# Five wq chunks kept between uses, and the place of w1 used for K, for wo and as three lent ring slots

## The chip, the cores and the metric

The kernel runs on one core of one Trainium2 chip. The metric is the device time of one execution in microseconds (us), as the median over runs. A profile of one execution stands beside it; its span runs from the first to the last instruction.

## What is computed

Two kinds of layer alternate, attention A and MLP B, twice each with the same weights, for one token of 1024 features, forward and backward:

```
x = A_x
x = x + A(layernorm(x));  x = x + B(layernorm(x))
x = x + A(layernorm(x));  x = x + B(layernorm(x))
A: q = x @ wq (32 heads of 128); scores against the last 4096 rows of k_cache (4 kv heads);
   softmax; sum over v_cache; @ wo
B: h = x @ w1 + b1;  act = h * tanh(softplus(h));  act @ w2
outputs: x, and the gradients of A_x, k_cache, v_cache, wq, wo, w1, b1, w2 for a given grad_out
```

wq is 1024 x 4096, wo 4096 x 1024, w1 1024 x 3584, w2 3584 x 1024, all bf16. The gradients of the two caches are full size (4 x 32768 x 128 each); all but the last 4096 rows of each are zeros.

## The kernel before

Weights pass through SBUF in chunks of 128 partitions x 4096 bf16, 1.05 MB each: wq and wo are eight chunks each, w2 seven. `ring_t` has eight such slots. K and V live whole in `KT` and `VS`, w1 whole in `W1` (128 x 8 x 3584, loaded as eight pieces of 0.92 MB). In the list below the number is the use: 0 first forward, 1 second forward (and wo's and w2's second use serve forward and backward both), 2 and 3 backward.

The class `Ring` (L40 to L80) sets the order of all loads. `want` appends a load to a list; `pump` walks the list in order and issues each load on SyncE's queue. A load with a place of its own (`own`: V, w1) is issued without a slot, any other takes the first free slot, and the walk stops when none is free. `release` gives a slot back and pumps, `keep` renames a chunk so that it stays for a later use. `release` is called while the program is being built, behind the instructions that use the chunk, and the loads that it lets go are put into the program at that point. The schedule is written out by hand: every engine runs its instructions in the order in which they were put, and waits between engines follow from who last wrote or read a place before that point.

The list (L254 to L270): K, q0, V, the first two w2 chunks (`EARLY_2`), o0, w1, the rest of w2, q1, o1, q2, w2 again, o3, q3. `KEEP_Q` (L251) names the wq chunks that stay from use 0 to use 1, `KEEP_Q2` (L252) those that stay from use 2 to use 3; q1 and q3 load only the others.

The stages, in order: K is transposed into `KT` (`kt_transposes`, L561, frees K's slots). `attn_fwd` (L462) multiplies wq chunk by chunk (L473), scores and softmax, then wo (L553); in the first attention each wo chunk is released after its products, in the second wo stays for the backward. `mlp_fwd` (L595) multiplies w1 (L601) and makes the activation `AC` (L628). Then w2 (L697 to L706): for each chunk the products forward (`mlp_out`, L653) and, in `rows_chunk` (L447), two blocks per chunk turned on TensorE (L431), evicted (L287 on ScalarE) and multiplied (L443) for the gradient; the other two blocks are row products on VectorE (L408). Products run two behind their transposes (`later`, L415), and a chunk's release is put behind its products, so a slot comes back at the end of the next chunk. The last w2 chunk is finished in `last_da` (L710), inside the second attention.

The backward runs `attn_bwd(1)` (wo, V, K, then wq in its `dn` part, L877 to L903), the second w2 stage (L1077 to L1082), `dn_b0` (L804, w1), and `attn_bwd(0)`. A wq chunk that was turned in use 2 and kept needs no turning in use 3 (`turned_q`, L893). From then on `W1` is used for rows and as staging: `stage_free` (L946) starts with three staging places in it, and VS, KT and the ring slots are added as they come free. Last, all weight gradients are made from rows (`work`), evicted into staging places and stored.

Zeros for the cache gradients, 56 stores of 1.05 MB, are issued on POOL's queue at fixed points (`zeros`, L240); with a second argument POOL first copies one word of that tile, so that it waits for it. `dn1` (L1123) has the last of them.

Of the kernel before, what the change touches and what calls it, by code (L numbers as in the profile page):

```python
# [15 lines left out]
P = 128  # L16
HQ = 32
DH = 128
D = 1024
# [6 lines left out]
TS = W // P  # L26
SLOT = 4096
# [10 lines left out]
class Ring:  # L38
# [12 lines left out]
    def pump(self):  # L51
        while self.pending:
            key, src, shape, own = self.pending[0]
            if own is None:
                if not self.free:
                    return
                s = self.free.popleft()
                n = 1
                for k in shape[1:]:
                    n *= k  # L60
                dst = self.slots[s][:, 0:n]
                if len(shape) == 3:
                    dst = dst.rearrange("p (a b) -> p a b", a=shape[1])
                self.where[key] = (s, dst)
            else:
                dst = own
            self.pending.popleft()
            self.nc.sync.dma_start(dst, src)

# [6 lines left out]

    def release(self, key):
        s, _ = self.where.pop(key)
        self.free.append(s)
        self.pump()  # L80


# [1 line left out]
def kernel(  # L84
# [50 lines left out]
    W1 = sb([P, TD, F], BF16, "W1")  # L135
# [56 lines left out]
    AC = sb([P, TF, 2], BF16, "AC")  # L192
# [13 lines left out]
    ring = Ring(nc, [ring_t[:, i, :] for i in range(8)])  # L206
    wq_v = A_wq.rearrange("(t p) j -> p t j", p=P)

    wo_v = A_wo.rearrange("(c p k) d -> p c k d", p=P, k=4)
# [3 lines left out]
    def kv_src(cache, g):  # L213
        return cache[0, g, ZR:, :].rearrange("(p t) d -> p t d", p=P)
# [2 lines left out]
        for t in ts:  # L217
            ring.want(("q", k, t), wq_v[:, t, :], [P, J])

    def want_o(k, cs=range(8)):  # L220
        for c in cs:
            ring.want(("o", k, c), wo_v[:, c], [P, 4, D])

    def want_2(k, cs=range(7)):
        for c in cs:
# [4 lines left out]
    for out_t in (out_2, out_3):  # L230
        for g in range(G):
            dst = out_t[0, g, 0:ZR, :].rearrange("(p r) d -> p (r d)", p=P).rearrange("p (r c) -> p r c", c=ZC)
# [7 lines left out]
    def zeros(n, after=None):  # L240

        if after is not None and zjobs:
            nc.gpsimd.tensor_copy(pz[0:1, pz_n[0] % 16:pz_n[0] % 16 + 1], after[0:1, 0:1])
            pz_n[0] += 1
        for _ in range(n):
            if zjobs:
                dst = zjobs.pop()
                nc.gpsimd.dma_start(dst, zt[:])  # L248


    KEEP_Q = (6, 7)  # L251
    KEEP_Q2 = (5, 6, 7)  # L252
    EARLY_2 = (0, 1)
    for g in range(G):  # L254
        ring.want(("K", g), kv_src(A_k_cache, g), [P, TS, P])
    want_q(0)
    for g in range(G):
        ring.want(("V", g), kv_src(A_v_cache, g), None, own=VS[:, g])
    want_2(0, EARLY_2)
    want_o(0)  # L260
    for t in range(TD):
        ring.want(("1", t), w1_v[:, t, :], None, own=W1[:, t, :])
    want_2(0, [c for c in range(7) if c not in EARLY_2])
    want_q(1, [t for t in range(8) if t not in KEEP_Q])
    want_o(1)
    want_q(2)
    want_2(1)
    want_o(3)
    want_q(3, [t for t in range(8) if t not in KEEP_Q2])
    ring.pump()  # L270
# [166 lines left out]
    def mv_open():  # L437

        fresh[0] = True
# [22 lines left out]
    def attn_fwd(l, x, st, first, wo_hook, q_hook=None):  # L462
# [7 lines left out]
        for t in range(TD):  # L470
            ch = ring.get(("q", l, t))
            for h in range(HQ):
                nc.tensor.matmul(q_ps[:, h:h + 1], lhsT=ch[:, h * P:(h + 1) * P], rhs=NA[:, t, l:l + 1],  # L473
                                 start=(t == 0 and h == 0), stop=(t == TD - 1), skip_group_check=True)
            if l == 0 and t in KEEP_Q:
                ring.keep(("q", 0, t), ("q", 1, t))
# [118 lines left out]
    def mlp_fwd(l, x, st):  # L595
        name = f"B{l}"
        n32, rstd = ln_fwd(x, st, NB[:, :, l], name)
        h_ps = MV[:, 192:192 + TF]
        for t in range(TD):
            for fb in range(TF):  # L600
                nc.tensor.matmul(h_ps[:, fb:fb + 1], lhsT=f_block(W1[:, t], fb), rhs=NB[:, t, l:l + 1],  # L601
                                 start=(t == 0 and fb == 0), stop=(t == TD - 1), skip_group_check=True)

        taken = []

        def col(n):
            if n == "mp":
                return sb([P, TF], FP32, f"{n}_{name}")
            taken.append(n)
            return mlp_t[:, (len(taken) - 1) * TF:len(taken) * TF]  # L610

        h, nh, z, w, m, om, A, B, num, den, t_, = (col(n) for n in "h nh z w m om A B num den t".split())
        V = nc.vector
        V.tensor_tensor(out=h[:], in0=h_ps, in1=b1c[:], op=ALU.add)

        V.scalar_tensor_tensor(out=nh[:], in0=h[:], scalar=-1.0, in1=h[:], op0=ALU.mult, op1=ALU.min)
        nc.scalar.activation(z[:], nh[:], ACT.Exp)
        nc.scalar.activation(w[:], nh[:], ACT.Exp, scale=2.0)
        V.tensor_scalar(out=m[:], in0=h[:], scalar1=0.0, scalar2=None, op0=ALU.is_ge)
        V.tensor_scalar(out=om[:], in0=h[:], scalar1=0.0, scalar2=None, op0=ALU.is_lt)  # L620
        V.tensor_tensor(out=A[:], in0=m[:], in1=w[:], op=ALU.max)
        V.tensor_tensor(out=B[:], in0=om[:], in1=w[:], op=ALU.max)
        V.scalar_tensor_tensor(out=num[:], in0=z[:], scalar=2.0, in1=A[:], op0=ALU.mult, op1=ALU.add)
        V.scalar_tensor_tensor(out=den[:], in0=B[:], scalar=2.0, in1=num[:], op0=ALU.mult, op1=ALU.add)
        V.reciprocal(den[:], den[:])
        V.tensor_tensor(out=t_[:], in0=num[:], in1=den[:], op=ALU.mult)
        if l == 0:
            V.tensor_tensor(out=AC[:, :, l], in0=h[:], in1=t_[:], op=ALU.mult)  # L628

        def deriv():  # L630

            mp, sg, s2 = col("mp"), col("sg"), col("s2")
            V.tensor_scalar(out=s2[:], in0=z[:], scalar1=1.0, scalar2=None, op0=ALU.add)
            V.reciprocal(s2[:], s2[:])
            V.tensor_tensor(out=sg[:], in0=m[:], in1=z[:], op=ALU.max)
            V.tensor_tensor(out=sg[:], in0=sg[:], in1=s2[:], op=ALU.mult)
            V.tensor_tensor(out=mp[:], in0=t_[:], in1=t_[:], op=ALU.mult)
            V.tensor_scalar(out=mp[:], in0=mp[:], scalar1=-1.0, scalar2=1.0, op0=ALU.mult, op1=ALU.add)
            V.tensor_tensor(out=mp[:], in0=mp[:], in1=h[:], op=ALU.mult)
            V.tensor_tensor(out=mp[:], in0=mp[:], in1=sg[:], op=ALU.mult)  # L640
            V.tensor_tensor(out=mp[:], in0=mp[:], in1=t_[:], op=ALU.add)
            return mp

        def act_late():
            V.tensor_tensor(out=AC[:, :, l], in0=h[:], in1=t_[:], op=ALU.mult)

        return dict(n32=n32, rstd=rstd, deriv=deriv, act_late=act_late)
# [36 lines left out]
    def early_da(k):  # L684
        c, tt = EARLY_2[k // 4], k % 4
        r = 4 * c + tt
# [6 lines left out]

    x1, st1, sA0 = attn_fwd(0, x0, st0, True, wo_hook0)
    sB0 = mlp_fwd(0, x1, st1)
    mp0 = sB0["deriv"]()
    y_ps = MV[:, 256:256 + TD]  # L697
    mv_open()
    for c in range(7):
        ch = ring.get(("2", 0, c))  # L700
        mlp_out(0, ch, c, y_ps)
        if c in EARLY_2:
            ring.release(("2", 0, c))
# [47 lines left out]
    dnp = sb([P, TD], FP32, "dnp")  # L751
# [52 lines left out]
    def dn_b0(g):  # L804
        bcast(lambda c: DHC[:, c, 0:1], STAY)
        mv_open()
        for t in range(TD):
            rowdot(W1[:, t, 0:STAY * P], [LB[0][:, 0:512]], 512, dnp[:, t:t + 1], True)
            mv(W1[:, t, STAY * P:], TF - STAY, TP[:, t:t + 1], lambda i: DHC[:, STAY + i, 0:1], True)
            if t == 2:  # L810
                rowize(GB, TD, 96, 0)
                take_back("AC", 96, NOFF)
                take_back("NB", 64, 0)
                take_back("OC", 32, NOFF)
                take_back("NA", 0, 0)
            if t == 4:
                rowize_f()
        return ln_bwd(dnp, sB0["n32"], sB0["rstd"], g, "B0")
# [107 lines left out]
    def dn3(t):  # L926
        if t % 2:
            w1_rest(1)
        if t == 5:
            zeros(1, dnp[:, t:t + 1])  # L930

    g2 = attn_bwd(1, sA1, g3, ("o", 1), ("q", 2), KEEP_Q2,
                  dict(do=lambda c: conv(2), dp=dp3, dq=dq3, dn=dn3))


    W1S = W1[:].rearrange("p t f -> p (t f)")
    ROWS = W1S[:, 0:5120]
    NOFF = 1024
    rf = W1S[0:7, 5120:6144]
    rt = W1S[0:64, 6144:6656].rearrange("p (k i) -> p k i", k=4)  # L940
# [2 lines left out]
    DOST = W1S[:, 11008:11264]  # L943

    TWIN = W1S[:, 11264:16384]
    stage_free = deque(W1S[:, 16384 + i * SLOT:16384 + (i + 1) * SLOT] for i in range(3))  # L946
    rt_n = [0]

    def rowize(cols, n, base, off):
# [136 lines left out]
    w1_rest(len(w1_units))  # L1086
    zeros(2, dh0)
    g1 = dn_b0(g2)
    nc.vector.tensor_copy(GA[:, :, 0], g1[:])
    zeros(2, g1)  # L1090

# [30 lines left out]

    def dn1(t):  # L1123
        if t in (3, 6, 7):
            zeros(2 if t < 7 else 1, dnp[:, t:t + 1])
        if t == 4:
            twins()
        if t == 5:
            todo[0].append(units_cols(0, 8, out_4))
# [9 lines left out]
    nc.vector.tensor_copy(g0b[:], g0[:])  # L1139
    store_rows(g0b[:], TD, out_1[0, 0, :])  # L1140
    stage_free.extendleft(ring_t[:, i, :] for i in range(8))

    way.close()
    late = ctx.enter_context(tc.tile_pool(name="late", bufs=1, space=bass.MemoryType.PSUM))
# [42 lines left out]
```

## Time and profile before

| | us |
|---|---|
| median of 3 runs | 462.74 (462.68 to 465.34) |
| span of the profiled execution | 460.6 |
| busy: TensorE / VectorE / ScalarE / GpSimd | 337.2 / 261.3 / 228.2 / 38.6 |

The core moved 183.59 MB (83.94 MB read from HBM, 98.62 MB written), 399 GB/s over the span; SyncE's queue carried 123.94 MB and POOL's queue, the zeros, 58.72 MB. The time around the profiled span is not listed; the median of the runs is 2.1 us above that span. In the profile, PE is TensorE, PEld its weight load, DVE VectorE, ACT ScalarE, SPq the instructions of SyncE's queue. The rows of a time line have the start, the duration, the engine, the line, what is written and read, a count, and in brackets the idle time before and what ended it. The granted clock is TensorE's, as a share of full speed. Many matmuls of a row are pipelined, and some records can be missing.

### The profile page before, as it was taken

Reading aid. Unit: us, or ns where it says so; the run is one execution under the profiler, and the core shown is the slowest. Engines: PE = TensorE matmul, PEld = TensorE weight load, DVE = VectorE, ACT = ScalarE, POOL = GpSimd, SP = SyncE. Lnnn points to the kernel's source line nnn. Section 1 sums busy time; section 2 is a strip of 40 time slices with the busy share of each in tenths; the row PEclk is TensorE's granted clock in tenths of the full one; section 3 lists DMA queues with packets and bytes.
Section 4 is the critical chain, followed back from the end, with each engine's and each line's share of the span. In section 5 each row is a group of like instructions: output and inputs, shape, how many; then the busy total and the mean of one; then the engine's idle time right before and its main releaser. Section 6 shows DMA issues by size and latency. Waiting matters only on the chain. (4 is left out here: it accounts for less than half of the span.)

```text
span 460.6 us, 14273 instructions
## 1 busy us (share of the span) xinstructions
PE 337.2 (73%) x6385; PEld 275.3 (60%) x6385; DVE 261.3 (57%) x517; ACT 228.2 (50%) x263; POOL 38.6 (8%) x85
## 2 busy tenths in 40 slices
PE   4836435597678788599879898897896876677950
PEld 3736435497668787599779898787791121112530
DVE  6505731383150149678428786475485987878860
ACT  2502001064035369378128573283267988778850
POOL 4000000000111320100210101102111000000000
PEclk9955555555555569799559855597595555555555
DMA  8999999999999999999999999979999999999995
GB/s 340 420 419 419 419 420 416 422 388 392 393 422 424 418 414 414 406 384 386 376 424 334 407 387 371 414 264 408 424 420 421 419 425 421 427 424 419 408 407 227
DMA packets 28379, 183.59 MB, mean 399 GB/s; under 512 B 3706, under 2 KB 3734, under 8 KB 9494
## 3 DMA queue, kind: packets, MB, share of 16 engines
q1 hardware_dynamic: 20162, 123.94, 67.0%
q0 software_dynamic: 8064, 58.72, 30.7%
q8 instruction: 50, 0.82, 0.7%
q14 instruction: 11, 0.09, 0.0%
q10 hardware_dynamic: 92, 0.02, 0.0%
HBM read 83.94 MB, written 98.62 MB: 396 GB/s over the span
## 5 line engine op out<-in xcount | busy, mean ns | idle before, releaser
L287 ACT COPY ring<-BIG 128x1024 bf16<-128x1024 bf16 x73 | 72.2, 1013 | 40.4 <-PE BIG L431 37.7
L431 PE MATMUL BIG<-ident_bf,ring 128*128 128x128 bf16 x872 | 80.0, 252 | 3.8 <-DMA ring<-in_A_wo_dram 2.0
L431 PEld LDWEIGHTS <-ring 128*128 128x128 bf16 x952 | 69.8, 114 | 5.2 <-DMA ring<-in_A_wo_dram 2.3
L995 PE MATMUL wide<-W 2*128 2x512 bf16 x228 | 48.5, 601 | 19.0 <-DVE ring L284 3.6
L408 DVE CUSTOM_DVE_ANT_0 junk<-ring,SC 128x1024 bf16<-128x1024 bf16 x38 | 46.2, 1216 | 4.5 <-DMA ring<-in_A_wo_dram 1.7
L995 PEld LDWEIGHTS <-W 2*128 2x128 bf16 x240 | 10.9, 103 | 54.5 <-issue 53.8
L443 PEld LDWEIGHTS <-ring 128*128 128x128 bf16 x1024 | 38.2, 100 | 4.6 <-ACT ring L287 4.4
L287 ACT COPY KT<-BIG 128x1024 bf16<-128x1024 bf16 x22 | 21.8, 1015 | 32.3 <-PE BIG L582 30.9
L287 ACT CAST ring<-wide 128x1024 bf16<-128x1024 f32 (+1 forms) x38 | 35.2, 998 | 4.9 <-PE wide L995 4.0
L284 DVE COPY ring<-BIG 128x1024 bf16<-128x1024 bf16 x36 | 24.8, 691 | 20.3 <-PE BIG L431 13.1
L284 DVE CAST ring<-wide 128x1024 bf16<-128x1024 f32 (+1 forms) x26 | 30.2, 1200 | 5.7 <-PE wide L995 5.2
L248 POOL DMA_DIRECT2D out_dram<-zt x56 | 29.6, 534 | 6.3 <-DMA out_dram<-zt 5.6
L553 PE MATMUL MV<-OC,ring 128*128 128x1 bf16 x512 | 16.6, 166 | 15.2 <-DMA ring<-in_A_wo_dram 12.6
L287 ACT COPY W<-BIG 128x1024 bf16<-128x1024 bf16 x20 | 18.9, 1151 | 15.7 <-PE BIG L766 15.7
L553 PEld LDWEIGHTS <-ring 128*128 128x128 bf16 x512 | 16.0, 106 | 16.0 <-DMA ring<-in_A_wo_dram 13.2
L284 DVE CAST VS<-wide 128x1024 bf16<-128x1024 f32 (+1 forms) x18 | 21.0, 1190 | 4.1 <-PE wide L995 3.1
L473 PE MATMUL MV<-NA,ring 128*128 128x1 bf16 x512 | 15.0, 165 | 10.9 <-DMA ring<-in_A_wq_dram 10.0
L601 PE MATMUL MV<-NB,W 128*128 128x1 bf16 x448 | 16.2, 172 | 9.2 <-DMA W<-in_B_w_dram 6.5
L408 DVE CUSTOM_DVE_ANT_0 junk<-ring,DSX 128x1024 bf16<-128x1024 bf16 x18 | 22.0, 1224 | 0.6
L601 PEld LDWEIGHTS <-W 128*128 128x128 bf16 x448 | 15.9, 118 | 9.8 <-DMA W<-in_B_w_dram 7.2
L1046 PE MATMUL wide<-W 32*128 32x256 bf16 x128 | 20.4, 403 | 1.4 <-ACT W L287 0.8
L473 PEld LDWEIGHTS <-ring 128*128 128x128 bf16 x512 | 14.3, 103 | 11.6 <-DMA ring<-in_A_wq_dram 10.6
(256 smaller groups left out, 539.1 us busy)
## 6 DMA issues: line engine op xcount, KB each, us to landing
out_dram<-zt POOLq DMA_DIRECT2D x56, 1024.0 KB, 12.7
ring<-in_A_wq_dram SPq DMA_DIRECT2D x27, 1024.0 KB
ring<-in_A_wo_dram SPq DMA_DIRECT2D x24, 1024.0 KB
ring<-in_B_w_dram SPq DMA_DIRECT2D x14, 1024.0 KB
out_dram<-ring SPq DMA_DIRECT2D x9, 1024.0 KB
W<-in_B_w_dram SPq DMA_DIRECT2D x8, 896.0 KB
ring<-in_A_k_cache_dram SPq DMA_DIRECT2D x4, 1024.0 KB
VS<-in_A_v_cache_dram SPq DMA_DIRECT2D x4, 1024.0 KB
```

Source lines behind the costliest of these rows:

```text
L248: nc.gpsimd.dma_start(dst, zt[:])
L284: nc.vector.tensor_copy(dst, src)
L287: nc.scalar.copy(dst, src)
L408: nc.vector.tensor_tensor_reduce(out=out, in0=a, in1=vec, scale=1.0, scalar=acc if i else 0.0, op0=ALU.mult, op1=ALU.add, accum_out=acc)
L431: nc.tensor.transpose(b[:, i * P:(i + 1) * P], block(w, i) if block else w[:, i * P:(i + 1) * P], ident_bf[:])
L443: nc.tensor.matmul(out, lhsT=w[:, i * P:(i + 1) * P], rhs=rhs_of(i), start=fresh[0], stop=last and i == n - 1, skip_group_check=True)
L473: nc.tensor.matmul(q_ps[:, h:h + 1], lhsT=ch[:, h * P:(h + 1) * P], rhs=NA[:, t, l:l + 1], start=(t == 0 and h == 0), stop=(t == TD - 1), ...
L553: nc.tensor.matmul(y_ps[:, dd:dd + 1], lhsT=ch[:, tt, dd * P:(dd + 1) * P], rhs=OC[:, h, l:l + 1], start=(h == 0 and dd == 0), stop=(h == ...
L601: nc.tensor.matmul(h_ps[:, fb:fb + 1], lhsT=f_block(W1[:, t], fb), rhs=NB[:, t, l:l + 1], start=(t == 0 and fb == 0), stop=(t == TD - 1), ...
L995: nc.tensor.matmul(b[:, 512 * i:512 * i + 512], lhsT=R[at:at + 2, lo:lo + P], rhs=R[at:at + 2, ro + 512 * i:ro + 512 * i + 512], start=Tru ...
L1046: nc.tensor.matmul(b[:, k * 256:(k + 1) * 256], lhsT=RT[32 * g:32 * g + 32, a, tp, :], rhs=YS[32 * g:32 * g + 32, :], start=True, stop=Tru ...
```

## The change

K is loaded into four of seven homes, 4096 columns each, that lie in `W1`, instead of into ring slots. The first seven chunks of o0 go into the same seven homes, the eighth into a ring slot. Both `KEEP_Q` and `KEEP_Q2` name five chunks. A load with its own place is now entered in `where`, and its release gives no slot back. After `dn_b0`, `ring.lend` adds three slots in `W1` (columns 16384 to 28671) to the ring; the staging list starts empty, and gets these three places at the end. Two zero stores are put after the first MLP's activation, and two fewer stand in `dn1`.

```diff
     def pump(self):
         while self.pending:
             key, src, shape, own = self.pending[0]
-            if own is None:
+            if own is not None:
+                self.where[key] = (None, own)
+                dst = own
+            else:
                 if not self.free:
                     return
                 s = self.free.popleft()
...
                 self.where[key] = (s, dst)
-            else:
-                dst = own
             self.pending.popleft()
             self.nc.sync.dma_start(dst, src)
...
     def release(self, key):
         s, _ = self.where.pop(key)
-        self.free.append(s)
+        if s is not None:
+            self.free.append(s)
+        self.pump()
+
+    def lend(self, slots):
+
+        self.free.extend(range(len(self.slots), len(self.slots) + len(slots)))
+        self.slots.extend(slots)
         self.pump()
...
-    def want_o(k, cs=range(8)):
+    def want_o(k, cs=range(8), homes=()):
         for c in cs:
-            ring.want(("o", k, c), wo_v[:, c], [P, 4, D])
+            own = homes[c].rearrange("p (k d) -> p k d", k=4) if c < len(homes) else None
+            ring.want(("o", k, c), wo_v[:, c], [P, 4, D], own)
...
-    KEEP_Q = (6, 7)
-    KEEP_Q2 = (5, 6, 7)
+    KEEP_Q = (3, 4, 5, 6, 7)
+    KEEP_Q2 = (3, 4, 5, 6, 7)
     EARLY_2 = (0, 1)
+    W1S = W1[:].rearrange("p t f -> p (t f)")
+    homes = [W1S[:, i * SLOT:(i + 1) * SLOT] for i in range(7)]
     for g in range(G):
-        ring.want(("K", g), kv_src(A_k_cache, g), [P, TS, P])
+        ring.want(("K", g), kv_src(A_k_cache, g), None, own=homes[g].rearrange("p (t d) -> p t d", t=TS))
     want_q(0)
     for g in range(G):
         ring.want(("V", g), kv_src(A_v_cache, g), None, own=VS[:, g])
     want_2(0, EARLY_2)
-    want_o(0)
+    want_o(0, homes=homes)
...
     sB0 = mlp_fwd(0, x1, st1)
+    zeros(2, AC[:, 0, 0:1])
...
-    stage_free = deque(W1S[:, 16384 + i * SLOT:16384 + (i + 1) * SLOT] for i in range(3))
+    lent = [W1S[:, 16384 + i * SLOT:16384 + (i + 1) * SLOT] for i in range(3)]
+    stage_free = deque()
...
     g1 = dn_b0(g2)
+    ring.lend(lent)
...
         if t in (3, 6, 7):
-            zeros(2 if t < 7 else 1, dnp[:, t:t + 1])
+            zeros(1, dnp[:, t:t + 1])
...
     stage_free.extendleft(ring_t[:, i, :] for i in range(8))
+    stage_free.extendleft(lent)
```

More of the change, by code (lines that the diff above doesn't have):

```diff
@@ L933 @@
                   dict(do=lambda c: conv(2), dp=dp3, dq=dq3, dn=dn3))
-    W1S = W1[:].rearrange("p t f -> p (t f)")
     ROWS = W1S[:, 0:5120]
```

## The prediction

> **What bounds the kernel now.** I read the page's first two parts, then a table by stretches, then the time lines of TensorE and of SyncE's queue between 60 and 120 us and around 260 to 310 us, where the ring of eight slots is used.
>
> ```profile
> PE 337.2 (73%) x6385; PEld 275.3 (60%) x6385; DVE 261.3 (57%) x517; ACT 228.2 (50%) x263; POOL 38.6 (8%) x85
> DMA  8999999999999999999999999979999999999995
> ```
>
> No engine is busy three quarters of the span, and the DMA engines are busy in every slice but the first and last and the one near 300 us. By stretches (columns: stretch, its length, busy us of PE, PEld, DVE, ACT, POOL, granted clock, DMA share, GB/s):
>
> ```profile
> 2.00:87.00 85.00, 45.29 (x1142) 42.03 (x1143) 32.53 (x75) 13.64 (x18) 4.15 (x4) 0.62 1.01 417
> 87.00:111.00 24.00, 19.47 (x454) 19.17 (x452) 17.04 (x50) 13.20 (x16) 0.00 (x0) 0.50 0.99 392
> 111.00:202.00 91.00, 71.25 (x1545) 66.03 (x1543) 37.60 (x116) 42.41 (x52) 15.63 (x32) 0.64 1.01 413
> 262.00:300.00 38.00, 34.61 (x699) 33.52 (x698) 26.53 (x63) 17.74 (x20) 2.47 (x6) 0.51 0.99 392
> 350.00:450.00 100.00, 70.57 (x394) 24.81 (x393) 77.67 (x69) 80.77 (x91) 0.00 (x0) 0.50 1.02 419
> ```
>
> Up to 87 us TensorE only follows the loads. From 87 to 350 us the order of the compute sets the pace, and DMA is full there because zero stores are handed out to fill it. From 350 us stores of 39.9 MB (98.62 MB written less 58.72 MB of zeros) set it. The time line of TensorE shows the place the change touches first:
>
> ```profile
> 69.29 1.01 PE L553 MATMUL MV<-OC,ring 128*128 128x1 bf16 x32 [1.47 <-DMA ring<-in_A_wo_dram]
> 72.73 2.01 PE L601 MATMUL MV<-NB,W 128*128 128x1 bf16 x56 [1.36 <-DVE NB L353]
> 75.83 1.09 PE L601 MATMUL MV<-NB,W 128*128 128x1 bf16 x28 [1.09 <-DMA W<-in_B_w_dram]
> 86.71 1.10 PE L601 MATMUL MV<-NB,W 128*128 128x1 bf16 x28 [1.08 <-DMA W<-in_B_w_dram]
> 90.21 2.70 PE L653 MATMUL MV<-AC,ring 128*128 128x1 bf16 x96 [2.41 <-DVE AC L628]
> 115.62 1.55 PE L473 MATMUL MV<-NA,ring 128*128 128x1 bf16 x52 [1.34 <-DMA ring<-in_A_wq_dram]
> ```
>
> wo's products (L553) end at 70.3, before w1's loads land, one each 2.18 us, the last at 86.7. The w2 stage starts at 90.2 with its chunks there. SyncE's issues:
>
> ```profile
> 60.76 8.83 SPq L68 DMA_DIRECT2D W<-in_B_w_dram  x8
> 71.48 20.08 SPq L68 DMA_DIRECT2D ring<-in_B_w_dram  x5
> 92.08 18.34 SPq L68 DMA_DIRECT2D ring<-in_A_wq_dram  x6
> ```
>
> **What goes.** Three loads of wq for the second forward use and two for the last: 5 x 1.05 MB, at the 420 GB/s of a loading stretch 12.5 us of DMA. That counts only if DMA is not left idle as long. Two zero stores move from L1125 to the first MLP; their bytes stay.
>
> **Step 1: what w1's place does to wo.** Loads are put into the program when `pump` runs. The first use of wq frees three slots. Two go to the early w2 chunks, the third to wo's eighth chunk; wo's first seven have homes in W1 and need no slot. So behind the third release nothing stops `pump`: w1's eight loads follow at once, before the products of wo stand in the program. In the kernel before, wo's last four loads needed slots that wo's own products freed, which put w1 behind them. Now those products (L553) read places that w1's loads wrote last by the program's order, so they must wait for these loads (and multiply w1's words). Home c holds parts of w1's chunks c and c+1. w1's loads themselves still wait only for wo's to land, which the stream orders anyway, so they land as before, the last at 86.7. wo's seventh chunk runs at 86.7, its eighth ends at 88.7 instead of 70.3. Behind it on TensorE are the norm and all of L601: norm 2.4 us (70.3 to 72.7), eight w1 chunks without waits 8.0 us (2.01 for two), activation 2.4 us (87.8 to 90.2). AC is ready at 101.5 instead of 90.15: **+11.4 us**. DMA idles meanwhile: w2's third chunk takes the eighth wo chunk's slot at 88.7, and nothing more is free. Cost bounds: 0 (if w1's loads waited for the products) and 11.4. I take 11.4, because L601's rows show that a reader of W1 waits for each load of what it reads.
>
> **Step 2: three slots in the first w2 stage.** Before, six circulated. A chunk's TensorE work is 3.0 us (rows at clock 0.5: 94.43, 97.46, 100.45), and its slot is given back at the end of the next chunk's. What a load takes from issue to use: the queue's row for the last wq load and the L473 row above give 110.09 to 115.62, 5.5 us; zero stores into a quiet queue land after 6.2 us.
>
> ```profile
> 110.09 0.33 SPq L68 DMA_DIRECT2D ring<-in_A_wq_dram  x1
> DMA to landing us min/median/max: 6.2/8.9/11.8
> ```
>
> I take 5.7 us for one alone. From AC at 101.5: the early chunks free slots at 102.6 and 103.5; the fourth and fifth chunk are loaded beside the two new zero stores (POOL's copy 0.67 us and 0.53 us each to issue; nothing waits on POOL until the second attention, L482). Each queue gets about half, as the four transfers are 10 us of data from 104: they land at 110.7 and 116. Then chunk by chunk: fourth 110.7 to 113.7 (frees the third's slot: sixth chunk at 119.5), fifth 116 to 119 (seventh chunk at 124.6), sixth 119.5 to 122.5 (wq's first), seventh from 124.6, norm and `last_da` to 131.3 as before (103.43 to 110.0). wq's second load is issued at 129, its third at 131.4 when `last_da` gives the last slot back: usable at 134.7 and 137. Five kept chunks follow at 0.9 us: q is done at 142.6 where it was 119.4. So +23.2 with step 1, **11.8 of it from the ring**. Bounds: without the zeros beside the loads the same walk ends at 138.2 (7.4); with every load 1 us longer at 146. Wo's loads for the second attention then start late too, but so does their use, by the same time.
>
> The Trainium skill, DMA: Bandwidth & Descriptors (Anatomy of one DMA), gives 2.0 us plus bytes over 436 GB/s, an estimate of 4.4 us for one chunk. By that, the two walks of this and the next step would shorten by about 6 us, and the sum below be 478; the row above has 5.5, and I stay with it.
>
> **111 to 262 us:** same instructions, same zeros, eight slots free for wo: only moved.
>
> **Step 3: three slots in the second w2 stage.** There wq's third use gives back three slots, not five:
>
> ```profile
> 260.67 0.95 PE L653 MATMUL MV<-AC,ring 128*128 128x1 bf16 x32
> 266.39 0.33 SPq L68 DMA_DIRECT2D ring<-in_B_w_dram  x1
> 275.06 1.22 DVE L408 CUSTOM_DVE_ANT_0 junk<-ring,SC 128x1024 bf16<-128x1024 bf16 x1 [1.58 <-DMA ring<-in_B_w_dram]
> ```
>
> The first release comes at 266.39, and that load, beside three zero stores, was usable 8.7 us later. Before, it was the sixth chunk; now it is the fourth, wanted at 269.2 and there at 274.5. The fifth (issued 269.4) follows at 277.5. The sixth is issued at 277.5 and there at 283.2, the seventh at 286.2, which started at 278.1 before: **+8.2 us** (6 if the zeros have drained first, 10 if all loads take 8.7).
>
> **Step 4: lent slots.** `lend` stands after the MLP's gradient; the loads are behind the row copies (L792 up to 294) on SyncE. wo's fourth to sixth chunk come about when wanted, the last two earlier than now: the waits of 0.62 and 1.40 us at 310.9 and 314.4 shrink. **-1** (0 to -2).
>
> **Step 5: two more wq chunks already turned.** Six transposes of 0.65 us with their evictions and three of DVE's 0.69 us copies go from 331 to 346; DVE's row products (1.27 us each) end the stage near 343.4: **-3** (-2 to -4).
>
> **Step 6: the tail.** Before, some 4.3 zero stores (10.5 us) were left at 350.2. Now two are gone and two wq loads fewer stand ahead, so they are through about when the first store can begin, 4.3 us after the norm. 39.9 MB at 420 GB/s are 95 us, then 5 us as before (455.5 to 460.6): 104.3 instead of 110.4, **-6.1**. ACT and DVE need about 80 us there and stay covered.
>
> **Sum:** 460.6 + 23.2 + 8.2 - 1 - 3 - 6.1 = 481.9 us span. The runs' median is 2.1 above the profiled span: **484**.
>
> **The rivals.**
> *A. wo's products are not held by w1* (the tracking lets them read first, w1's loads wait for them). For it: the layout reads as if meant so; against it: the order of `pump`. Step 1 is 0 and step 2 stays: 484 - 11.4 = **473**. Chance 0.15.
> *B. Faster: DMA stays the bound.* The share of 0.99 to 1.01 speaks for it. If the two zero stores and the loads cover every stall, 462.7 - 12.5 = **450**. It decides if DMA's added idle time stays below some 8 us; step 1 alone has 5 us around 87 and 11 from 93 to 104. Chance 0.09.
> *C. Even:* w1 is not held and loads come 2 us quicker, so that the ring costs 12 instead of 20: 473 - 8 = **465**, and with the tail 2 us shorter within 1%. Against it stand the 5.5 us of the row above. Chance 0.06.
>
> **How the numbers follow.** The forecast has 0.70. Its own range is 476 (step 2 at 7.4 and step 3 at 6, together 6.6 less, and 2 more for the tail) to 490 (both at their upper ends, 5.2 more). To leave out no more than 2 in 10 the range reaches down over A and its spread to C's value, with 2 more above: **465 to 492**. Within 1% is about what a measurement can tell from no change. Faster by over 1%: B, 0.09. Within 1%: C, 0.06. Slower: the forecast and A, 0.85.
>
> **What would show it.** Step 1: L553's last product near 88 us, waiting on DMA of W, and L601 without waits. Step 2: DMA share well below 1 between 87 and 140, L653 waiting on loads of w2, the second QC copy near 142. Step 3: the same waits in the second w2 stage, its last chunk 8 us later than its first would give. Step 5: fewer L431 products before the norm. Wrong would be: L553 ending at 70 (A), or DMA share near 1 up to 140 us (B).

## The result and the profile after

The changed kernel takes 491.24 us (median of 4 runs, 488.88 to 492.0) where the kernel before took 463.77 beside it: a ratio of 1.0617, 95% interval 1.0554 to 1.0679. Its profiled span is 490.2 us against 460.6. The first two parts of its page:

```profile
PE 334.7 (68%) x6337; PEld 271.1 (55%) x6337; DVE 260.3 (53%) x515; ACT 224.6 (46%) x259; POOL 38.7 (8%) x86
DMA  8999999267699899999999967799999899899998
```

TensorE, VectorE and ScalarE did slightly less, GpSimd the same, and 178.33 MB moved instead of 183.59. What is new are two holes in the row of the DMA engines, the 8th to 11th slice and the 24th to 26th. In the table by stretches (length, busy us of PE, PEld, DVE, ACT, POOL, granted clock, DMA share, GB/s) the first is the late w1 products with the w2 stage behind them, the second is the second w2 stage:

```profile
87.00:111.00 24.00, 13.98 (x390) 13.50 (x386) 7.11 (x33) 4.05 (x7) 1.33 (x3) 0.50 0.51 185
111.00:142.00 31.00, 19.57 (x486) 19.02 (x487) 11.31 (x26) 10.94 (x12) 0.00 (x0) 0.50 0.74 276
290.00:330.00 40.00, 28.66 (x603) 27.73 (x602) 22.22 (x56) 13.73 (x15) 2.48 (x6) 0.50 0.83 304
```

In the time line of TensorE (line numbers have moved: L553 is now L564, L601 is L612, L653 is L664, L473 is L484):

```profile
49.47 0.34 PE L338 MATMUL TP<-junk,ident_bf 128*32 128x8 bf16 x16 [0.89 <-DVE junk L548]
71.37 0.91 PE L564 MATMUL MV<-OC,W 128*128 128x1 bf16 x28 [21.56 <-DMA W<-in_B_w_dram]
86.61 0.90 PE L564 MATMUL MV<-OC,W 128*128 128x1 bf16 x28 [1.24 <-DMA W<-in_B_w_dram]
87.37 0.99 PE L564 MATMUL MV<-OC,ring 128*128 128x1 bf16 x32
90.79 7.60 PE L612 MATMUL MV<-NB,W 128*128 128x1 bf16 x224 [1.36 <-DVE NB L364]
100.80 2.70 PE L664 MATMUL MV<-AC,ring 128*128 128x1 bf16 x96 [2.41 <-DVE AC L639]
112.35 1.01 PE L664 MATMUL MV<-AC,ring 128*128 128x1 bf16 x32 [7.13 <-DMA ring<-in_B_w_dram]
121.53 1.01 PE L664 MATMUL MV<-AC,ring 128*128 128x1 bf16 x32 [3.05 <-DMA ring<-in_B_w_dram]
134.12 1.02 PE L484 MATMUL MV<-NA,ring 128*128 128x1 bf16 x32 [2.15 <-DMA ring<-in_A_wq_dram]
136.62 4.10 PE L484 MATMUL MV<-NA,ring 128*128 128x1 bf16 x148 [1.48 <-DMA ring<-in_A_wq_dram]
143.23 1.31 PE L484 MATMUL MV<-NA,ring 128*128 128x1 bf16 x44 [2.51 <-issue]
```

The second row is the reading that matters: products of wo (they read OC) wait 21.56 us for a load whose source is w1. All but wo's last chunk read the place W after w1 was written there, so seven of its eight chunks are multiplied as w1's words: this kernel leaves out the order that would keep wo's data until they are read. L612 then finds its eight chunks ready. From 112 us on TensorE waits for single loads of w2 and wq, where the profile before had one such wait in this stretch. The second w2 stage shows the same:

```profile
299.96 1.01 PE L664 MATMUL MV<-AC,ring 128*128 128x1 bf16 x32 [5.19 <-DMA ring<-in_B_w_dram]
308.21 1.01 PE L664 MATMUL MV<-AC,ring 128*128 128x1 bf16 x32 [2.12 <-DMA ring<-in_B_w_dram]
312.00 1.01 PE L664 MATMUL MV<-AC,ring 128*128 128x1 bf16 x32 [0.64 <-DMA ring<-in_B_w_dram]
```

Where the 29.6 us of span come from, by the starts of VectorE's rows that end each stage (first column: the row's tile):

| stage ends with | before | after | stage longer by | forecast |
|---|---|---|---|---|
| AC, first activation | 89.96 | 100.55 | 10.6 | 11.4 |
| QC, second attention | 119.40 | 144.58 | 14.6 | 11.8 |
| GB, second w2 stage begins | 259.98 | 285.64 | 0.5 | 0 |
| dh, second w2 stage ends | 282.83 | 316.73 | 8.2 | 8.2 |
| DQC, last wq stage begins | 328.91 | 363.39 | 0.6 | -1 |
| g0b, last wq stage ends | 349.21 | 382.48 | -1.2 | -3 |
| end of the span | 460.6 | 490.2 | -3.7 | -6.1 |

The profiled execution of the changed kernel is the slowest of the four (492.0 us), so the span is 8.3 us above the forecast's 481.9, and the median 7 us above its 484.

### The profile page after: what moved, and what is told of

Read it like the earlier page. It is cut to its first block, busy times and chain, and to the rows that moved or that the text cites. A ratio compares the mean times of both kernels' runs of the same rounds, so it can differ in the third digit from the quotient of the medians.

```text
span 490.2 us, 14134 instructions
## 1 busy us (share of the span) xinstructions
PE 334.7 (68%) x6337; PEld 271.1 (55%) x6337; DVE 260.3 (53%) x515; ACT 224.6 (46%) x259; POOL 38.7 (8%) x86
## 2 busy tenths in 40 slices
DMA packets 27658, 178.33 MB, mean 364 GB/s; under 512 B 3626, under 2 KB 3654, under 8 KB 9414
## 3 DMA queue, kind: packets, MB, share of 16 engines
q0 software_dynamic: 8064, 58.72, 29.6%
## 5 line engine op out<-in xcount | busy, mean ns | idle before, releaser
L298 ACT COPY ring<-BIG 128x1024 bf16<-128x1024 bf16 x62 | 61.4, 1013 | 56.0 <-PE BIG L442 54.0
L442 PE MATMUL BIG<-ident_bf,ring 128*128 128x128 bf16 x720 | 68.1, 257 | 2.4 <-ACT W L298 1.1
L442 PEld LDWEIGHTS <-ring 128*128 128x128 bf16 x776 | 59.3, 117 | 3.5 <-issue 2.9
L419 DVE CUSTOM_DVE_ANT_0 junk<-ring,SC 128x1024 bf16<-128x1024 bf16 x34 | 41.3, 1215 | 11.7 <-DMA ring<-in_B_w_dram 10.5
L1007 PEld LDWEIGHTS <-W 2*128 2x128 bf16 x240 | 10.6, 103 | 52.4 <-issue 52.0
L298 ACT COPY KT<-BIG 128x1024 bf16<-128x1024 bf16 x22 | 21.7, 1015 | 34.9 <-PE BIG L593 33.4
L454 PEld LDWEIGHTS <-ring 128*128 128x128 bf16 x896 | 33.4, 101 | 6.8 <-ACT ring L298 4.9
L298 ACT COPY W<-BIG 128x1024 bf16<-128x1024 bf16 x28 | 26.6, 1112 | 19.9 <-PE BIG L778 16.3
L257 POOL DMA_DIRECT2D out_dram<-zt x56 | 29.7, 536 | 7.1 <-DMA out_dram<-zt 6.0
L295 DVE COPY ring<-BIG 128x1024 bf16<-128x1024 bf16 x28 | 19.4, 691 | 19.4 <-PE BIG L442 12.5
L564 PE MATMUL MV<-OC,W 128*128 128x1 bf16 x224 | 7.2, 166 | 30.5 <-DMA W<-in_B_w_dram 30.5
L664 PE MATMUL MV<-AC,ring 128*128 128x1 bf16 x448 | 13.7, 165 | 20.5 <-DMA ring<-in_B_w_dram 18.1
L484 PE MATMUL MV<-NA,ring 128*128 128x1 bf16 x512 | 15.3, 165 | 14.6 <-DMA ring<-in_A_wq_dram 12.1
L664 PEld LDWEIGHTS <-ring 128*128 128x128 bf16 x448 | 13.1, 104 | 21.2 <-DMA ring<-in_B_w_dram 18.7
L564 PEld LDWEIGHTS <-W 128*128 128x128 bf16 x224 | 6.6, 104 | 31.1 <-DMA W<-in_B_w_dram 31.1
L484 PEld LDWEIGHTS <-ring 128*128 128x128 bf16 x512 | 14.4, 103 | 15.3 <-DMA ring<-in_A_wq_dram 12.7
L295 DVE CAST VS<-wide 128x1024 bf16<-128x1024 f32 (+1 forms) x17 | 19.7, 1186 | 5.0 <-PE wide L1007 4.2
L298 ACT CAST KT<-wide 128x1024 bf16<-128x1024 f32 x20 | 20.2, 1022 | 4.2 <-PE wide L1007 3.1
```

Of the source, the lines that this page charges most:

```text
L295: nc.vector.tensor_copy(dst, src)
L298: nc.scalar.copy(dst, src)
L419: nc.vector.tensor_tensor_reduce(out=out, in0=a, in1=vec, scale=1.0, scalar=acc if i else 0.0, op0=ALU.mult, op1=ALU.add, accum_out=acc)
L442: nc.tensor.transpose(b[:, i * P:(i + 1) * P], block(w, i) if block else w[:, i * P:(i + 1) * P], ident_bf[:])
L454: nc.tensor.matmul(out, lhsT=w[:, i * P:(i + 1) * P], rhs=rhs_of(i), start=fresh[0], stop=last and i == n - 1, skip_group_check=True)
L564: nc.tensor.matmul(y_ps[:, dd:dd + 1], lhsT=ch[:, tt, dd * P:(dd + 1) * P], rhs=OC[:, h, l:l + 1], start=(h == 0 and dd == 0), stop=(h == ...
```

## The experiments

The theory: products of wo wait for w1 because of the order in which loads enter the program, and a ring of three slots makes two stages wait for single loads; both lie on the path and add up. Rivals: only the ring matters and hides the wait for w1; or the amount of DMA work sets the time. Intervals below are at 95%, each against the kernel before on the same chip, 460.7 to 461.4 us there.

**e1_order: w1 behind wo's products.**

```diff
+        self.read = 0
...
             key, src, shape, own = self.pending[0]
+            if key[0] == "1" and self.read <= min(6, (3584 * key[1] + 3583) // 4096):
+                return
...
         s, _ = self.where.pop(key)
+        self.read += s is None and key[0] == "o"
```

> The changed kernel, but each load of w1 is put into the program only after wo's products of the homes that it overwrites (in the changed kernel wo's first seven products are made with w1's words; here with wo's). Theory (the wait of wo's products for w1 and the waits of the short ring add up on the path): L564's row in this kernel ends near 70 us, the first w2 products start near 90 instead of 101 us, the stage behind is moved 10.6 us forward, 480.5 us. Rival (what sets the time is the ring alone, and the wait for w1 is covered by it): no change, 491. Rival (DMA work sets the time): no change either, since the bytes are the same.

480.72 us, ratio 1.0419 (1.0377 to 1.046). Its time line of TensorE (L568 is L564, L668 is L664 and L488 is L484 of the changed kernel):

```profile
69.41 1.01 PE L568 MATMUL MV<-OC,ring 128*128 128x1 bf16 x32 [1.46 <-DMA ring<-in_A_wo_dram]
102.35 1.01 PE L668 MATMUL MV<-AC,ring 128*128 128x1 bf16 x32 [7.57 <-DMA ring<-in_B_w_dram]
111.77 1.01 PE L668 MATMUL MV<-AC,ring 128*128 128x1 bf16 x32 [3.29 <-DMA ring<-in_B_w_dram]
```

wo ends at 70.4 again, AC is at 90.10, and everything behind is earlier: AC and QC by 10.5 and 10.3 us, the rows after them by 8.9 to 10.5, the end of the span by 10.5 (479.7 against 490.2). The ring's waits are as long as before. The wait for w1 is a term of its own; both rivals fall.

**e2_homes and e3_order_homes: two and three chunks kept**, without and with the order of e1.

```diff
-    KEEP_Q = (3, 4, 5, 6, 7)
-    KEEP_Q2 = (3, 4, 5, 6, 7)
+    KEEP_Q = (6, 7)
+    KEEP_Q2 = (5, 6, 7)
```

> The changed kernel with two and three wq chunks kept as before; the homes, the lent slots and the zeros stay as in the change (wo's first seven products are again made with w1's words). Theory: the 10.6 us of the wait for w1 remain, the two ring waits (14.6 and 8.2 us) go, the tail stays some 3 us shorter than before: 471 us, with w2's products not waiting on loads. Rival (ring alone): about 464, as before.

> Both taken back: w1's loads behind wo's products, two and three chunks kept; homes, lent slots and zeros as in the change. Theory: nothing is left that costs, 460 to 465 us; the two earlier zero stores push wq's loads back by up to 5 us and shorten the tail by about as much. Rival (the homes, or the lent slots, cost by themselves): over 467.

e2: 466.37 us, 1.0111 (1.0088 to 1.0134). e3: 457.61 us, 0.992 (0.9895 to 0.9945). Between them lies the wait for w1 without a short ring, 8.8 us by the medians and 9.2 by the spans: nearly the 10.5 of e1. e2 came out under its expectation for two reasons: more of the tail went than thought (106.2 us from g0b to the end of the span, where 111.4 less 3 was expected), and from QC to GB it takes 137.9 us where the kernel before takes 140.6. The expectation for e3 was missed to the same side. Why QC to GB is shorter was not tried. Against the kernel before, nothing is left that costs; e3 is even quicker by a little under 1%. Homes and lent slots are harmless in themselves.

**e4_order_q2 and e5_order_q: one ring alone**, e3 with five chunks kept in one place. e4:

```diff
-    KEEP_Q2 = (5, 6, 7)
+    KEEP_Q2 = (3, 4, 5, 6, 7)
```

> As e3_order_homes, but five chunks kept between uses 2 and 3. Theory: against e3_order_homes +8.2 us in the second w2 stage, -1.6 us in the last wq stage, and 0 to -3 us in the tail: 4 to 7 us slower than it, about 468. Rival (two loads of wq fewer shorten the time by their DMA time): 5 us faster than it.

e5 does the same in the other place:

```diff
-    KEEP_Q = (6, 7)
+    KEEP_Q = (3, 4, 5, 6, 7)
```

> As e3_order_homes, but five chunks kept between uses 0 and 1. Theory (each ring wait counts by itself): the first w2 stage ends as in e1_order, the second attention's q 11 us later than in e3_order_homes, nothing else slower: 457.6 + 11 = 469 us. Rival (three loads fewer give back their DMA time further on): 461 or less.

e4: 468.22 us, 1.0159 (1.0119 to 1.0199), 10.6 us over e3 instead of 4 to 7; that the expected total of 468 came is luck, since e3 was itself quicker than thought. The second w2 stage (GB to dh) is 7.6 us longer than e3's, as thought; what was not: wo's stage behind it, from dh to the copy into DOC, is 2.2 us longer (three ring slots and three lent ones, against five and three in e3), of which 0.9 is left at DQC; the last wq stage gives nothing back against e3's (19.6 against 19.7 us), and in the tail 1.6 us are added. e5: 472.25 us, 1.0241 (1.0191 to 1.0292), 14.6 over e3 instead of 11: q of the second attention is the expected 11.4 later (134.29 against 122.91), and from there to GB it takes 141.5 us against 137.7, where no difference was expected. Of these 3.8 us some 1.7 are longer stops of TensorE that the profile marks "issue" (on them see below); the rest was not followed. Two and three loads fewer save nothing in either.

**e11_keep6_q2: two slots**, the suspected wait increased. Against e3:

```diff
-    KEEP_Q2 = (5, 6, 7)
+    KEEP_Q2 = (2, 3, 4, 5, 6, 7)
```

> As e3_order_homes, but six wq chunks kept between uses 2 and 3, so two slots circulate in the second w2 stage. Theory: each of the five later chunks is asked for when the chunk before its turn ends, and is waited for in full, 5.5 to 6 us each: that stage 27 to 32 us longer than in e3_order_homes instead of 9 with five kept; with the turning saved some 480 to 487 us. Rival (a fixed loss by the number of kept chunks): 4 us more than e4_order_q2, 472.

491.29 us, 1.0648 (1.0608 to 1.0688). The w2 products from the third chunk on:

```profile
277.05 1.01 PE L668 MATMUL MV<-AC,ring 128*128 128x1 bf16 x32 [7.70 <-DMA ring<-in_B_w_dram]
285.09 1.01 PE L668 MATMUL MV<-AC,ring 128*128 128x1 bf16 x32 [4.90 <-DMA ring<-in_B_w_dram]
293.17 1.01 PE L668 MATMUL MV<-AC,ring 128*128 128x1 bf16 x32 [4.93 <-DMA ring<-in_B_w_dram]
301.39 1.01 PE L668 MATMUL MV<-AC,ring 128*128 128x1 bf16 x32 [5.08 <-DMA ring<-in_B_w_dram]
309.53 1.01 PE L668 MATMUL MV<-AC,ring 128*128 128x1 bf16 x32 [5.00 <-DMA ring<-in_B_w_dram]
```

One chunk now takes 8.1 us: 3.0 of work and one load's whole way, from its issue to its use. The same work in windows over this stage, of e3 (five slots), e4 (three) and e11 (two):

```profile
260.60:284.00 23.40, 21.87 (x456) 21.63 (x456) 17.55 (x31) 14.07 (x14) 1.77 (x4) 0.52 1.01 404
```

```profile
261.50:292.50 31.00, 21.87 (x456) 21.46 (x456) 17.57 (x31) 14.07 (x14) 1.75 (x4) 0.53 0.76 277
```

```profile
263.00:314.00 51.00, 22.45 (x456) 21.89 (x456) 17.38 (x29) 13.97 (x14) 1.76 (x4) 0.51 0.48 169
```

456 matmuls and some 22 us of TensorE each time, in 23, 31 and 51 us, while the DMA share halves. The 27.9 us over e3 are within what was expected; the total is 4 us above, since wo's stage (dh to DQC), with five slots left, is 5.4 us longer as well. A loss fixed per kept chunk is ruled out: the sixth costs 20.3 us in this stage, where the fourth and fifth together cost 7.6.

**e7_keep4 and e9_keep3: four slots, and five in the first ring.** e7 against e3:

```diff
-    KEEP_Q = (6, 7)
-    KEEP_Q2 = (5, 6, 7)
+    KEEP_Q = (4, 5, 6, 7)
+    KEEP_Q2 = (4, 5, 6, 7)
```

> As e3_order_homes, with four chunks kept both times, so that four slots circulate. Theory: a load asked for at the end of chunk c+1 has two chunks of work, 6 us, until its chunk's turn, and takes 5.5 to 6 us alone, so nearly all the waiting goes: 1 us in the first w2 stage, 1 to 3 in the second, 0 to 2 in the tail: 459 to 463 us. Rival (the waits grow in proportion to the chunks kept): two thirds of the way to five kept, over 470.

e9 is e3 with one chunk more in the first place alone:

```diff
-    KEEP_Q = (6, 7)
+    KEEP_Q = (5, 6, 7)
```

> As e3_order_homes, but three wq chunks kept between uses 0 and 1, so five slots circulate there. Theory: a wait comes only from three slots on; one load fewer in a stage that the loads set takes up to 2.5 us off: 455 to 458 us. Rival (each kept chunk costs its share, 14 us over three chunks): 462.

e7: 462.23 us, 1.001 (0.9971 to 1.0048). e9: 457.86 us, 0.9934 (0.9907 to 0.9962). e7 is as quick as the kernel before, but 4.6 us behind e3, and the intervals of these two do not overlap. From AC to QC it takes 34.9 us against e3's 32.8, from GB to dh 25.0 against 23.4. So four slots cost some 2 us in each ring stage; three cost 11.3 (e5) and 7.6 (e4). Most of the loss begins between four and three: with four, a load has two chunks of work, 6 us, for its way of 5 to 6 us, with three only one. The load that e9 saves shortens nothing against e3.

**e6_zeros_back: the two zero stores of the changed kernel at their old place.**

```diff
-    zeros(2, AC[:, 0, 0:1])
...
-            zeros(1, dnp[:, t:t + 1])
+            zeros(2 if t < 7 else 1, dnp[:, t:t + 1])
```

> The changed kernel with the two zero stores at their old place (wo's first products with w1's words, as in the change). Theory: without them the fourth and fifth w2 chunk come 3 to 4 us earlier, and so does the second attention; the tail, which after the change has idle DMA time because evictions set it, takes the two stores in that idle time: 2 to 4 us faster than the changed kernel, 487 to 489. Rival (DMA sets the tail): the tail grows by 5 us, 1 to 2 us slower.

486.37 us, 1.0565 (1.0487 to 1.0644); the interval overlaps that of the changed kernel, so the traces have to tell. QC of the second attention is at 138.45 instead of 144.58, 6.1 us earlier: AC is ready at the same time in both (100.55 and 100.67), and the fourth w2 chunk's product begins at 112.35 with the zeros and, in e6, without them at 106.87:

```profile
106.87 1.01 PE L664 MATMUL MV<-AC,ring 128*128 128x1 bf16 x32 [1.53 <-DMA ring<-in_B_w_dram]
```

The zeros cost here and give nothing back later. The tail, from g0b to the end of the span, is 107.7 us in both. Its first 96 us, in the changed kernel and in e6:

```profile
382.50:478.50 96.00, 70.49 (x389) 24.34 (x390) 74.77 (x68) 80.07 (x91) 0.00 (x0) 0.50 0.96 390
```

```profile
376.00:472.00 96.00, 70.48 (x389) 24.32 (x390) 74.76 (x68) 80.06 (x91) 0.00 (x0) 0.50 1.00 406
```

The same evictions on DVE and ACT in the same time, with DMA at 0.96 and at 1.00: the two stores only fill idle time, so DMA does not set the pace there. What does are the evictions with the products they wait for.

**e8_zeros_alone, e12_no_zeros and e10_zeros4: what makes e3 quicker.** e8 is the kernel before with the two stores moved, which are these two lines of the change:

```diff
+    zeros(2, AC[:, 0, 0:1])
...
-            zeros(2 if t < 7 else 1, dnp[:, t:t + 1])
+            zeros(1, dnp[:, t:t + 1])
```

e12 is e3 with the same two lines taken back. e10 is e3 with four stores behind the first activation and one in `dn1`:

```diff
-    zeros(2, AC[:, 0, 0:1])
+    zeros(4, AC[:, 0, 0:1])
...
-        if t in (3, 6, 7):
+        if t == 7:
             zeros(1, dnp[:, t:t + 1])
```

> The kernel before, with the two zero stores moved to the first MLP and nothing else. Theory: the tail's backlog is what e3_order_homes saved: q of the second attention some 3.5 us later, made up by the time of the second MLP, and the tail 5 us shorter: 456 to 459 us. Rival (homes or lent slots gained it): 461, as before.

> As e3_order_homes, with the two zero stores back at their old place: homes and lent slots alone. Theory: the lent slots save the waits for wo in the last backward, 1 to 2 us; the tail is 3 to 5 us longer than in e3_order_homes, q of the second attention 3.5 us earlier: 459 to 461 us. Rival (the whole gain comes from the zeros): 461, as the kernel before.

> As e3_order_homes, with four instead of two zero stores after the first activation and one instead of three in the last wq stage. Theory: the evictions already set the tail there, so nothing more is to be had from it, and the loads of the first w2 stage come 5 us later: 459 to 463 us. Rival (DMA sets the tail): 457.6 or less.

e8: 459.45 us, 0.9977 (0.9943 to 1.0011), not told apart from the kernel before. e12: 458.21 us, 0.9943 (0.9921 to 0.9965), quicker than its expectation of 459 to 461, since its tail is only 0.7 us longer than e3's instead of 3 to 5. e10: 462.48 us, 1.0041 (1.0014 to 1.0068). The theory that the moved stores gained e3's time falls: e12 keeps most of it without them. What goes with the gain in e12 is one hole filled; the DMA engines between 300 and 318 us in the kernel before and in e12:

```profile
300.00:318.00 18.00, 14.85 (x355) 14.17 (x353) 12.12 (x22) 13.23 (x15) 0.70 (x2) 0.94 0.87 317
```

```profile
300.00:318.00 18.00, 15.36 (x347) 14.73 (x345) 12.32 (x25) 12.73 (x15) 0.71 (x3) 0.91 1.01 411
```

What DMA does there with three lent slots is not left over at the end, I read from this; no run lends the slots by themselves. The tail (before: 111.4) is 106.6 us in e12, 105.9 in e3 and 105.9 in e10, which moved two stores more and only made the first w2 stage later. About 106 us is the least that any of the twelve shows, and the evictions end 96 us into the tail in all of these, the kernel before among them.

## Why the prediction was right or wrong

The direction, the mechanism and the places were right: slower, by a wait of wo's products for w1 and two waits of a short ring. The range of 465 to 492 holds 491.24, at its upper end; the likeliest case's own range, up to 490, does not. The forecast of 484 is 7 us short.

What failed are sizes of terms in the sum. The largest miss is Step 2: five kept chunks in a row were put at 0.9 us each, with nothing for a stop of TensorE, and the term came to 14.6 us instead of 11.8. The next is Step 6: it took the evictions of the tail as covered by DMA, and 3.7 us were gained instead of 6.1. Steps 5 and 4 gave 1.8 and 1.6 us less than forecast, the stretch put at nothing (QC to GB) cost 0.5, and only Step 1 was too high, by 0.8.

*Step 1* said 11.4 us, and 10.6 came: w1's loads landed as before, L564's last product ended at 88.4 where 88.7 was forecast, and L612 took 7.6 us instead of 8.0. e1 gives it back alone. Rival A (w1 held behind wo) is what e1 is, not what the change is.

*Step 2* said 11.8 us, and 14.6 came. The walk from chunk to chunk ended as forecast, the third wq load usable at 136.62 against 137, but in part by luck: two sizes on the way were off and cancelled. The load that was to share DMA with the zero stores did not share at first: the two stores of L257, issued by POOL at 100.9 and 101.6, took from issue to landing (least, median, most)

```profile
DMA to landing us min/median/max: 5.0/7.7/10.4
```

The first went as if alone: from 101.8 to 105.4 us the DMA engines moved packets of the stores' queue only, and from 105.4 to 110.6 the two queues shared evenly (47.6% and 49.1% of the engines' time). So the fourth chunk, asked for at 101.82, came 10.5 us later instead of 8.1, at 112.35 where 110.7 was forecast. Against that the fifth chunk was there by 115.36 (forecast 116), and the second and third wq loads took 5.3 and 5.4 us instead of 5.7. What was missing in the sum comes after the walk: the five kept chunks in a row met a stop of TensorE, the 2.51 us "issue" at 143.23 above, where the kernel before lost 0.9. e1 and e5 show it at 1.9 in the same line, e6 at 2.1.

The traces say what such stops follow. A packet of 16 KB on the queue for instructions (q8) moved from 141.00 to 141.88, and TensorE went on at 143.23, 1.35 us after it. In the time lines of all fourteen kernels TensorE has 81 stops of 0.8 us or more marked "issue", and every one ends 1.2 to 1.6 us after such a packet. I read them as TensorE waiting for its next instructions; no run changes how these are loaded.

*Step 3* said 8.2 us and has 8.2; e4 and e11 confirm how it grows.

*Step 4* said a gain of 1 us; 0.6 was lost up to DQC. The forecast had counted the slots that are lent, not that the ring in front has two fewer: TensorE waits 2.2 us for loads of wo here, about as long as before (2.0), where e12, with five ring slots and the lent ones, has no such wait. The price was too high as well: with that wait gone, the stage of e12 and e3 is only 0.1 and 0.5 us shorter than before.

*Step 5* said 3 us gained; 1.2 came. It let VectorE run without waits from the start, and it took three of VectorE's copies away where two went (eight before, six after). The row products stand behind the copies of the first chunks, so they begin only 8.2 us after DQC (before: 7.4), and from there VectorE runs to the last of them with one gap of 0.3 us.

*Step 6* said 6.1 us gained; 3.7 came. What failed is its last sentence: that evictions need 80 us and stay covered. They are busy for that long, but with the products they wait for they take 96 to 98.6 us, and under less DMA work this chain is the bound: more or fewer zero stores no longer change the tail (e6 and e10).

Put right, the terms give 460.6 + 10.6 + 14.6 + 0.5 + 8.2 + 0.6 - 1.2 - 3.7 = 490.2, the span. *Rival B* (DMA stays the bound) failed at the point named for it: the share of 0.51 between 87 and 111 us means some 12 us idle in that stretch alone. *Rival C* did not come about, since w1 did hold wo's products and the loads were at most 0.9 us quicker than the 5.7 taken.

The Trainium skill, DMA: Bandwidth & Descriptors (Anatomy of one DMA), would have had one load at 4.4 us, an estimate from its formula, which it gives for transfers that GpSimd issues. In e11, where each load is alone, it took from issue to use 4.8 us:

```profile
280.27 0.33 SPq L72 DMA_DIRECT2D ring<-in_B_w_dram  x1
```

against the L668 row at 285.09. That is nearer to the page than to the 5.7 us that I took; but the time came out above the forecast, and the sum by the page, 478, was below it, so it would have been further off.

Two things stay open. With five chunks kept in the second place the evictions of the tail end 98.6 us after g0b instead of 96 (97.5 with four, 97.2 with six), with nearly the same busy times; no run shows why. And whether the stops of TensorE would go if its instructions came sooner was not tried.

## What to carry to other kernels

When a load gets a place of its own instead of a slot from a pool, look at what the slot was holding back: here it kept w1's loads behind the reads of wo in the program, and without it the reads waited for the wrong data, 10.5 us. Count slots in a ring by time: a load needs its whole way from the release to the use. Here, with releases one chunk late, 3 us of work per chunk and some 5 us of way, four slots cost some 2 us a stage, three cost 8 to 11, two cost 28. Bytes saved were worth nothing in stages that wait for the way of single loads, and at the end no more than until the next bound, the evictions with their products. The version to keep is e3, 0.8% quicker than the kernel before: the homes and lent slots, with the old number of kept chunks and w1 held back.

## What the runs showed of the hardware

A load alone on the DMA engines was used 4.8 to 5.0 us after its issue (e11), though 1.05 MB are 2.5 us of data at the 420 GB/s of a loading stretch: by this estimate half of its time is not data.

A load issued 0.9 us after a zero store on the other queue (100.93 and 101.82) had no packet until 105.8, 4.0 us later; in e1, with the same order, the load issued at 91.38 had its first at 95.5. Without the stores (e6) a load issued at 101.94 had its first packet at 102.9. Once the load had begun, the two queues shared evenly.

TensorE stops for up to 2.5 us in the changed kernel's second attention with nothing to wait for that the profile names (2.51 and 2.22), each time until 1.3 us after a packet of instructions has come.
